# Computing one chunk's decays with one-column matmuls in place of two transfers through DRAM, in a fused recurrence and bilinear feed-forward kernel

## The chip, the cores and the metric

One core of one Trainium2 chip. The metric is the time of one launch on the device in microseconds (us). Ratios compare runs of the state "fast" alone; the medians of the table of experiments are over all timed runs, slow ones included. A "look" is one profiled execution; a look without timed rounds has the state "unknown". The profile's span is some 2 us shorter than the time of the same run.

## The reference, cut to what matters

```python
def _attn_ref(q, k, v, alpha):            # 4 x 8 heads x 768 steps x 48
    state = zeros((B, H, D, D))
    for t in range(S):
        state = alpha[:, :, t, :, None] * state + einsum('bhd,bhe->bhde', k[:, :, t], v[:, :, t])
        y[:, :, t] = einsum('bhd,bhde->bhe', q[:, :, t], state)
    return y

def _moe_ref(x, w_a, w_b, w_out):         # 3072 x 384, d_ff = 1536
    return ((x @ w_a) * (x @ w_b)) @ w_out

# the first feeds the second: x = y with heads side by side
```

The kernel cuts the 768 steps into stretches and works through six chunks (two batch rows by 256 steps each). Inside a chunk the recurrence is done by matmuls with scaled keys and queries. From one half of a chunk to the next, the state is multiplied by the half's **decay**, the product of its alphas: 48 numbers for each head. This text is about how chunk 3's decays get from where they are computed to where the state is scaled.

## The kernel before, where the change and the argument touch it

There are two routines for the same numbers. One takes them from beta (computed already) by two transfers, because they stand in two rows and are needed in columns. The other sums the logarithms again with matmuls against a column of ones, whose result already stands in columns, and takes the exponential on ScalarE:

```python
def decay(ch):                                        # "dec D"
    row = dram.tile([2, B, P2, D], F32, name="row")
    for r in range(2):
        nc.sync.dma_start(out=row[r]..., in_=ch.beta[HC - 1::HC, :, 1, ...]...)      # L213
    for r in range(2):
        nc.sync.dma_start(out=bls[ch.c % 2][r * DP:r * DP + D]..., in_=row[r]..., allow_slow_non_contiguous=True)   # L216

def decay_pe(ch):                                     # "dec P"
    s2 = bank("s2", 1, F32, [C, 2, 512])              # the one s bank
    for u in range(2):
        for hd in range(H):
            r, p = hd // P2, hd % P2
            for g in range(2):
                ...
                nc.tensor.matmul(s2[r * DP:r * DP + D, g, e:e + 1], lhsT=ch.l2[gs, u, hd, :], rhs=one[gs], start=True, stop=True)   # L228
    for r in range(2):
        nc.scalar.activation(out=bls[ch.c % 2][rs]..., in_=s2[rs, :, :2 * P2], func=AF.Exp)   # L231
```

The 32 matmuls of decay_pe are called "the burst" below. The user of the decays is the end of stK ("K"), which makes the state of the chunk's middle, Sm, and of its end, S; stS ("S") needs Sm, and stY ("Y") finishes the chunk's output, in two halves, Y0 and Y1. Y also reads m, the product with a mask that stage "D" (L273, L274) makes on VectorE:

```python
# stK: state of the chunk's middle (Sm) and of its end (S)
for g, (src, dst) in enumerate(((old, mid), (mid, new))):
    ...
    nc.vector.tensor_add(tmp[:, us], x, src)          # L341, x in PSUM (the s bank)
    eng.tensor_mul(dst, tmp[:, us], bl)               # L342, both inputs in SBUF

# stS: first half of the queries against S, second half against Sm, no wait between but for Sm
for g in range(...):
    st = Sm[...] if g else S0[...]
    ...matmul(y[...], lhsT=win(st[rs], a, t), rhs=queriesT(...))      # L291

# logs, "L": for the next chunk but one, on ScalarE and then GpSimd ("P")
nc.scalar.activation(out=x, in_=x, func=AF.Ln)        # L170
eng.tensor_add(ch.l2..., x[:, :, 0, :], x[:, :, 1, :])   # L172, reads SBUF twice
```

A plan says at which step of one chunk's feed-forward (24 half products ff_a, ff_b, then 4 outputs) a stage of another chunk is issued. The part that counts, during the feed-forward of chunk 2:

```python
2: [(1, 3, "v * S"), (3, 4, "ld a * P"), (4, 4, "ld k * P"), (5, 3, "dec D"), (6, 3, "D 0 0 y2"), (7, 3, "K * V"), (7, 4, "L * P"),
    (8, 3, "T 1 Y"), (9, 3, "S 0"), (9, 3, "D 0 1 s2"), (13, 3, "Y 0 VS"), (13, 3, "D 1 0 s2"), (14, 4, "A 0"), ...
```

Chunks 0, 1 and 2 already use "dec P", chunks 3, 4 and 5 "dec D".

## Time and profile before

| | before |
|---|---|
| time, median of the first 3 runs (range) | 219.32 us (218.82 to 219.59) |
| profiled span | 217.3 us |
| TensorE busy | 200.0 us, 92% |
| waits of TensorE after 96 us | one, 2.23 us, for Sm of chunk 3 |
| from Y1 of chunk 2 to Y0 of chunk 3 | 18.26 us |

The lines themselves are in the prediction below. The last row is the measure that I use all through: the distance between the starts of two groups of matmuls (L309 at 93.86 and at 112.12 us in the timeline of before). All that happens earlier in the run drops out of it. That matters: in the fourteen profiles of this study the first of these two groups starts anywhere from 92.73 to 95.14 us in kernels that are alike, or nearly so, up to there, so 2.4 us of the spread of these profiles comes from the first part of the run, which the change doesn't touch.

### The profile page before, as it was taken

How to read it: one execution, taken by the hardware profiler on the slowest of the kernel's cores; microseconds unless marked ns; L12 is line 12 of the kernel's file. 1: busy time of each engine (PE TensorE's matmuls, PEld its weight loads, DVE VectorE, ACT ScalarE, POOL GpSimd, SP SyncE). 2: the span in 40 equal slices, each digit the busy share in tenths (PEclk: the TensorE clock that was granted, in tenths of full speed). 3: DMA queues.
4: the chain of work that ended last, by engine and by line, in shares of the span. 5: the costliest groups of instructions: out<-in, count | busy, mean ns of one | idle time of the engine just before them, and what ended most of it. 6: DMA issues, size and time to landing. Idle time of an engine off the chain costs nothing.

```text
span 217.3 us, 6393 instructions
## 1 busy us (share of the span) xinstructions
PE 200.0 (92%) x2762; PEld 118.2 (54%) x2762; DVE 129.0 (59%) x208; ACT 119.8 (55%) x208; POOL 54.0 (25%) x66
## 2 busy tenths in 40 slices
PE   7767898999899989999599999999999999999992
PEld 7556664556565645654355555554655545544462
DVE  4668736797646879906778908559554463045500
ACT  8853276943488977248339635875433433244421
POOL 8575948029400057000620000700100000000000
PEclk9999999999999999999889999999999999999999
DMA  7999999998999355994697257595328100320023
GB/s 166 263 251 126 212 224 226 245 250 219 304 264 288 102 100 129 262 200 95 102 251 186 56 114 80 77 266 86 63 50 159 36 3 0 91 57 0 0 64 81
DMA packets 40607, 31.24 MB, mean 144 GB/s; under 512 B 29036, under 2 KB 36740, under 8 KB 40580
## 3 DMA queue, kind: packets, MB, share of 16 engines
q0 software_dynamic: 9120, 19.27, 38.8%
q1 hardware_dynamic: 31380, 11.48, 27.3%
q8 instruction: 21, 0.34, 0.7%
q10 hardware_dynamic: 80, 0.10, 0.1%
q14 instruction: 6, 0.05, 0.1%
HBM read 25.97 MB, written 4.74 MB: 141 GB/s over the span
## 4 chain that ended last, share of the span: by engine, by line
PE 69%; DMA 8%; ACT 7%; DVE 6%; SPq 3%; POOL 3%; issue 3%; DVEq 0%; ACTq 0%
PE f L382 19%; PE f L359 18%; PE f L369 17%; PE y L309 4%; PE y L291 3%; DMA k_t<-in_k_dram 3%; DVE m L274 3%; DMA wb_t<-in_moe_w_b_dram 3%; PE f L196 2%; PE s L273 2%; SPq L163 2%; ACT L170 1%; DMA bl<-row 1%; ACT a_t L170 1%; DVE QKp L207 1%
## 5 line engine op out<-in xcount | busy, mean ns | idle before, releaser
L359 PE MATMUL f<-xT,wa_t 128*128 128x512 bf16 (+1 forms) x240 | 60.2, 361 | 1.7 <-ACT as__745 L363 0.8
L369 PE MATMUL f<-xT,wb_t 128*128 128x512 bf16 (+1 forms) x240 | 60.1, 361 | 0.5 <-DMA wb_t<-in_moe_w_b_dram 0.5
L382 PE MATMUL f<-wo_t,prod 128*128 128x384 bf16 (+1 forms) x300 | 49.5, 320 | 0.0
L382 PEld LDWEIGHTS <-prod 128*128 128x128 bf16 x300 | 28.3, 98 | 18.1
L359 PEld LDWEIGHTS <-wa_t 128*128 128x128 bf16 x240 | 22.2, 98 | 24.2 <-issue 3.1
L369 PEld LDWEIGHTS <-wb_t 128*128 128x128 bf16 x240 | 22.7, 98 | 22.5 <-issue 1.7
L274 DVE TENSOR_TENSOR m<-s,mask 128x1024 bf16<-128x1024 f32 x22 | 26.9, 1222 | 6.0 <-PE s L273 5.9
L383 ACT ACTIVATE ot<-f 128x384 f32<-128x384 f32 (+1 forms) x25 | 11.9, 478 | 32.1 <-PE f L382 32.1
L172 POOL TENSOR_TENSOR l<-a_t 128x768 f32<-128x768 f32 x3 | 5.4, 1808 | 67.3 <-ACT a_t L170 67.3
L207 DVE TENSOR_TENSOR QKp<-q_t,beta 128x384 bf16<-128x384 f32 x24 | 12.9, 578 | 0.6 <-ACT beta L201 0.6
L299 ACT ACTIVATE xT<-y 128x384 bf16<-128x384 f32 (+1 forms) x12 | 7.8, 651 | 9.2 <-DVE xT L297 4.7
L207 DVE TENSOR_TENSOR QKp<-k_t,invb 128x384 bf16<-128x384 f32 x24 | 12.2, 553 | 0.2
L309 PE MATMUL y<-m,vx 64*64 64x128 bf16 x576 | 10.4, 218 | 1.7 <-DVE m L274 1.7
L309 PEld LDWEIGHTS <-vx 64*64 64x64 bf16 x576 | 8.8, 107 | 5.1 <-issue 4.9
L273 PE MATMUL s<-kqT 64*64 64x128 bf16 x352 | 10.6, 224 | 0.7 <-DVE kqT L252 0.7
L196 PE MATMUL f<-l,ut_f 128*128 128x384 f32 x24 | 9.2, 498 | 2.1 <-DVE l L172 1.1
L178 ACT ACTIVATE vx<-v_t 128x768 bf16<-128x768 f32 x10 | 8.0, 844 | 5.3 <-DMA v_t<-in_v_dram 5.3
L291 PE MATMUL y<-kqT,Sm 64*64 64x128 bf16 x144 | 6.7, 226 | 4.3 <-DVE Sm L342 2.2
L273 PEld LDWEIGHTS <-kqT 64*64 64x64 bf16 x384 | 7.6, 108 | 4.3 <-issue 2.7
L170 ACT ACTIVATE a_t<-a_t 128x1536 f32<-128x1536 f32 (+1 forms) x7 | 9.1, 1300 | 1.0 <-DMA a_t<-in_alpha_dram 0.9
L189 PE MATMUL f<-ident 128*128 128x128 bf16 x102 | 8.0, 249 | 1.4 <-POOL ident masks.py:199 1.4
L189 PEld LDWEIGHTS <-ident 128*128 128x128 bf16 x102 | 7.3, 114 | 1.5 <-POOL ident masks.py:199 1.4
(227 smaller groups left out, 267.0 us busy)
## 6 DMA issues: line engine op xcount, KB each, us to landing
out_dram<-ot SPq DMA_DIRECT2D x47, 96.0 KB, 2.2
a_t<-in_alpha_dram POOLq DMA_DIRECT2D x5, 768.0 KB, 8.5
k_t<-in_k_dram POOLq DMA_DIRECT2D x4, 768.0 KB, 12.2
q_t<-in_q_dram POOLq DMA_DIRECT2D x4, 768.0 KB, 7.5
v_t<-in_v_dram POOLq DMA_DIRECT2D x4, 768.0 KB, 10.7
wo_t<-in_moe_w_out_dram POOLq DMA_DIRECT2D x3, 384.0 KB, 10.8
a_t<-in_alpha_dram SPq DMA_DIRECT2D x2, 384.0 KB, 4.4
k_t<-in_k_dram SPq DMA_DIRECT2D x2, 384.0 KB
```

The source lines that it names most:

```text
L170: nc.scalar.activation(out=x, in_=x, func=AF.Ln)
L189: nc.tensor.matmul(w[:, :C], lhsT=ident, rhs=ident, start=True, stop=True)
L196: nc.tensor.matmul(p, lhsT=ut_f32, rhs=ch.l2[:, u].rearrange("p h d -> p (h d)"), start=True, stop=True)
L207: eng.tensor_mul(dst[ch.c % 2][:, u, :, i::2, :D], src[:, u, hs].rearrange("p a r d -> p r a d"), by[:, u, :, hs])
L273: nc.tensor.matmul(s2[g * HC:(g + 1) * HC, r, p, rk, :], lhsT=keysT(ch, u, 2 * h + p, g, r, rk), rhs=queriesT(ch, u, 2 * h + p, g, rs), st ...
L274: nc.vector.tensor_mul(m.rearrange("p r a k s -> p (r a) (k s)"), s2.rearrange("p r a k s -> p (r a) (k s)"), maskn(4))
L291: nc.tensor.matmul(y[rs, g, t * C:(t + 1) * C], lhsT=win(st[rs], a, t), rhs=queriesT(ch, u, a, g, rs), start=(n == 0), stop=False, skip_gr ...
L309: nc.tensor.matmul(ch.y[u][r * DP:(r + 1) * DP, g, t * C:(t + 1) * C], lhsT=win(vxs[ch.c % 2][gs, u, rk], a + P2 * r, t), rhs=ch.m[u, a // ...
L359: nc.tensor.matmul(ap, lhsT=wa_t[:, kk, f * 128:(f + 1) * 128], rhs=ff_x(ch, us)[:, kk], start=(kk == 0), stop=(kk == KT - 1))
L369: nc.tensor.matmul(bp, lhsT=wb_t[:, kk, f * 128:(f + 1) * 128], rhs=ff_x(ch, us)[:, kk], start=(kk == 0), stop=(kk == KT - 1))
L382: nc.tensor.matmul(op, lhsT=ch.prod[:, f, m * C:(m + 1) * C], rhs=wo_t[:, f, fs], start=(f == 0), stop=(f == NFF - 1))
L383: nc.scalar.activation(out=ot[:, fs], in_=op, func=AF.Copy)
```

## The change

Its intent: take the two transfers in series off the way to chunk 3's middle state. It is one word of the plan.

```diff
-    2: [... (4, 4, "ld k * P"), (5, 3, "dec D"), (6, 3, "D 0 0 y2"), (7, 3, "K * V"), (7, 4, "L * P"),
+    2: [... (4, 4, "ld k * P"), (5, 3, "dec P"), (6, 3, "D 0 0 y2"), (7, 3, "K * V"), (7, 4, "L * P"),
```

## The prediction

> **What bounds the kernel now.** I read the busy times and the row of slices first, then TensorE's waits from 96 us to the end, then the timeline around the one wait found there.
>
> ```profile
> PE 200.0 (92%) x2762; PEld 118.2 (54%) x2762; DVE 129.0 (59%) x208; ACT 119.8 (55%) x208; POOL 54.0 (25%) x66
> PEclk9999999999999999999889999999999999999999
> ```
>
> TensorE is busy 200.0 of 217.3 us. The clock row dips to 8 in only two slices of 5.43 us, the twentieth and the next, that is, from about 103 to 114 us. In TensorE's list of waits over the second half of the span there is one entry:
>
> ```profile
> PE y L291 <- DVE Sm L342: 2.2, 1, 2.2
> ```
>
> So TensorE sets the end, and from 96 us on it idles once, for the middle state of chunk 3 (Sm = tmp x decay). Time given back there should reach the end, as long as no new wait eats it. The timeline (start, length, engine, instruction; idle before it in brackets):
>
> ```profile
> 99.71 1.18 SPq L213 DMA_DIRECT2D row<-beta  x2
> 101.42 0.93 SPq L216 DMA_DIRECT2D bl<-row  x2
> 103.45 0.55 DVE L341 TENSOR_TENSOR tmp<-s,S 128x384 f32<-128x384 f32 x1
> 104.40 0.52 PE L291 MATMUL y<-kqT,S 64*64 64x128 bf16 x12
> 104.88 1.80 POOL L172 TENSOR_TENSOR l<-a_t 128x768 f32<-128x768 f32 x1 [19.29 <-ACT a_t L170]
> 104.97 2.12 DVE L342 TENSOR_TENSOR Sm<-tmp,bl 128x384 bf16<-128x384 f32 x1 [0.97 <-DMA bl<-row]
> 107.15 0.85 PE L291 MATMUL y<-kqT,Sm 64*64 64x128 bf16 x12 [2.23 <-DVE Sm L342]
> 107.79 0.56 DVE L342 TENSOR_TENSOR S<-tmp,bl 128x384 bf16<-128x384 f32 x1
> 108.39 1.46 PE L359 MATMUL f<-xT,wa_t 128*128 128x512 bf16 x3
> ```
>
> Three things add up. VectorE had tmp at 104.00 but waited 0.97 us for the second transfer. That delay put Sm just behind GpSimd's add (104.88 to 106.68), and Sm took 2.12 us where the next multiply of the same shape took 0.56; it ended 0.41 us after the add. And after the idle time TensorE is slow: three matmuls of L359 take 1.46 us (usually 0.81). The table by windows, whose last columns are granted clock, DMA share and GB/s, shows why:
>
> ```profile
> 106.00:107.00 1.00, 0.00 (x0) 0.00 (x0) 1.00 (x1) 0.00 (x0) 1.00 (x2) 1.00 1.16 211
> 108.00:109.00 1.00, 1.00 (x18) 0.50 (x11) 1.00 (x3) 0.00 (x0) 1.00 (x2) 0.50 0.54 63
> 110.00:111.00 1.00, 1.00 (x5) 0.42 (x4) 0.08 (x1) 0.48 (x1) 0.08 (x1) 0.73 1.05 313
> ```
>
> The clock is halved from 107.1 to about 110.5 us. So the wait costs more than its 2.23 us.
>
> **What the Trainium skill says.** "TensorE: Matmul & The Clock Gate", Part 1, says that the array's clock is halved after an idle window and comes back after about 3.4 us of work. The trace agrees on the halving and on the 3.4 us, though the idle stretch here was 2.23 us, less than a whole such window. "SBUF — State Buffer", section "SBUF: two separate sides", says that a VectorE operation with two SBUF inputs and a GpSimd operation that reads SBUF lock each other out, and whichever starts first has the port to its end. The trace agrees (2.12 against 0.56 us). [...] here issue to landing of row and bl is 3.4 us in the median, so two in series cannot be short. Removing them is right in kind.
>
> **The change part by part.** One word changes, but it moves the work: chunk 3 uses the other decay routine.
>
> *Removed:* four issues on the sync queue, the landing wait of 0.97 us and, through it, the collision.
>
> *Added on TensorE:* 32 fp32 matmuls of 64x48 by one column, which the trace splits into 64, at the place where ff_a of step 6 begins in the old program (100.50 us). The same burst for chunk 2 in the trace of before:
>
> ```profile
> 70.24 0.81 PE L359 MATMUL f<-xT,wa_t 128*128 128x512 bf16 x3
> 70.98 1.16 PE L228 MATMUL s<-one,l 64*48 64x1 f32 x64
> 72.07 0.82 PE L369 MATMUL f<-xT,wb_t 128*128 128x512 bf16 x3
> ```
>
> From its start to the next group is 1.09 us; and a group of three FF matmuls before such a burst takes 0.74 start to start, not 0.65. So it costs 1.09 + 0.09 = **1.18 us**, all on the path.
>
> *Added on ScalarE:* two exponentials, 0.178 us each by the row of L231. The order of the changed program has them after as_ of step 5 and ahead of the next as_, and no added table load. TensorE reaches the next as_ about 0.8 us after the burst, so they hide. They must also free the s bank before K (chunk 3's state products), which starts two FF groups and a D later, over 1.5 us. They hide there too.
>
> *Moved:* everything on TensorE, ScalarE and GpSimd here comes 1.18 us later. tmp then ends at 104.00 + 1.18 = 105.18, Sm follows at once and ends at about 105.72. The add starts at 104.88 + 1.18 = 106.06, so Sm misses it by 0.34 us. TensorE starts its S part at 105.58 and needs Sm 0.36 us later, at 105.94. **No wait.**
>
> *What the removed wait gave.* Before, from the S part at 104.40 to the start of Y0 (L309) at 112.12 is 7.72 us. What stands between is S and D (unstalled 1.02 us: chunk 4's, from 115.18 to the next FF group at 116.20) and four FF groups (3 x 0.65 + 0.74 = 2.69): 3.71 us. So idle and slow clock cost 7.72 - 3.71 = 4.01 us. Less 1.18, Y0 could come **2.83 us** earlier, if nothing else held it.
>
> *What is given back.* VectorE does not move with TensorE here. After Sm come the second tmp (to about 106.39) and then S = tmp x bl at 106.42, which has two SBUF inputs and now starts 0.36 us after the add. As Sm did before, it should end 0.41 us after the add: 106.68 + 1.18 + 0.41 = 108.27, beside 108.35 in the old trace. So VectorE's next operations (prod 0.68, then the mask multiply m 1.22, overlapping slightly) stand at the same absolute times as before, m ending at about 110.01. Y0 reads that m first. TensorE wanted it at 105.58 + 3.71 = 109.29; it gets it at 110.07. New waits of about 0.78 us in all appear (part of it perhaps a step earlier, at the bank that prod frees). Y0 thus comes at 110.07 instead of 112.12: **2.05 us** earlier. Later I find slack again: m of D 1 1 should end at about 115.55 and Y1 is wanted at 115.60.
>
> The sum: 4.01 - 1.18 - 0.78 = 2.05, so 219.32 - 2.05 = **217.3 us**, 0.9% faster.
>
> **The rivals.** *A: the clock drops anyway*, by its own schedule or for the thinness of the one-column bursts. Then only the 2.23 us of idle time are saved against 1.18, and with any new wait the gain is 0.3 to 1.0 us: 218.3 to 219.0. Against it: the bursts of chunks 1 and 2 ran at a clock of 1.00 before and after, and the only drop inside the run stands just behind the 2.23 us gap. A gap of 1.7 us near 56 us (L291 for tmp) left the clock at 1.00.
>
> *B: no new wait.* If S comes before the add, or VectorE's backlog is shorter than I think, the full 2.83 us stay: 216.5. For it: there are only 0.36 us between add and S in my sum, and instructions on VectorE overlap. Against it: the add hangs on a logarithm that shifts with TensorE by the same 1.18.
>
> *C: the collision only moves to Sm.* If ScalarE does its logarithm 0.4 us earlier against TensorE than I have it, the add meets Sm again; Sm would then end at about 107.9 and TensorE would idle some 2 us, perhaps with a slow clock. Then the matmuls are pure cost: up to 1.2 us slower, 220.5. Against it: ScalarE's as_ ahead of the logarithm waits for TensorE's own products.
>
> *D: a later transfer becomes the wait.* GpSimd issues the loads of chunks 4 and 5 after the add, now 1.18 us later, with users 2 us earlier. v of chunk 4 is cast at 122.98; issued at 107.79, with a landing of 10.7 us in the median, it would be there by about 119.7 after the change and wanted at about 120.9. The margin is 1.2 us; a miss on ScalarE would be a part of a microsecond, not of TensorE's time at once.
>
> **Range and chances.** B gives 216.5, my sum 217.3, A 218.3 to 219.0, C 220.5 with a small chance. The three timed runs span 0.8 us. A range of 216.2 to 218.5 should hold it 8 times in 10. A gain above 2% needs 214.9, more than all of idle time and slow clock less the matmuls: 2 in 100. A loss above 2% needs 223.7: 1 in 100.
>
> **What would show it right or wrong.** In the changed profile: L228 has 64 more matmuls on TensorE and L213 and L216 have eight issues, not twelve; the wait of L291 for Sm is gone; Sm takes 0.56 us and S of chunk 3 about 1.9; the clock row stays at 9; and L309 of chunk 3 shows a new wait of 0.4 to 0.8 us for m. A clock that still dips makes A right; S at 0.56 us and no wait of L309 makes B right; Sm again at 2 us makes C right. A TensorE wait traced to a load after 115 us would mean D, and none of my sums.

## The result, and the profile after

| | before | after |
|---|---|---|
| time, median | 219.07 us (4 runs, 217.99 to 219.59) | 216.58 us (4 runs, 216.55 to 217.09) |
| ratio, 95% interval | | 0.990 (0.986 to 0.994) |
| profiled span | 217.3 us | 214.7 us |
| from Y1 of chunk 2 to Y0 of chunk 3 | 18.26 us | 16.23 us |
| from Y0 of chunk 3 to the end | 105.2 us | 104.9 us |

A ratio here is the mean time of one kernel's fast runs over that of the other's in the same rounds, so it isn't quite the ratio of the medians. By the 2% rule this is "the same": the change gains 1.0%.

TensorE's granted clock in slices, and its list of waits from 96 us to the end, after:

```profile
PEclk9999999999999999999999999999999999999999
```
```profile
PE y L309 <- DVE m L274: 0.3, 1, 0.3
```

The dip in the clock row is gone, the wait for Sm is gone, and a small wait that was not there before has come: Y0 (L309) for the mask multiply m. The timeline of the changed kernel at the same place:

```profile
100.33 1.16 PE L228 MATMUL s<-one,l 64*48 64x1 f32 x64
101.54 0.37 ACT L231 ACTIVATE bl<-s 48x16 f32<-48x16 f32 x2 [1.15 <-PE s L228]
104.97 0.56 DVE L342 TENSOR_TENSOR Sm<-tmp,bl 128x384 bf16<-128x384 f32 x1
105.69 0.50 PE L291 MATMUL y<-kqT,Sm 64*64 64x128 bf16 x12
105.81 1.81 POOL L172 TENSOR_TENSOR l<-a_t 128x768 f32<-128x768 f32 x1 [20.48 <-ACT a_t L170]
106.22 1.82 DVE L342 TENSOR_TENSOR S<-tmp,bl 128x384 bf16<-128x384 f32 x1
108.56 1.21 DVE L274 TENSOR_TENSOR m<-s,mask 128x1024 bf16<-128x1024 f32 x1
109.82 0.86 PE L309 MATMUL y<-m,vx 64*64 64x128 bf16 x48 [0.33 <-DVE m L274]
```

Sm now takes 0.56 us and is over at 105.53, before GpSimd's add begins at 105.81. The S half of the same pair of products runs into the add instead and takes 1.82 us; the mask multiply stands behind it, and Y0 behind that.

So of 2.6 us between the two profiles, 2.03 us lie in the stage of the change. The rest is not the change's: 0.27 us were there before it (the first group starts at 93.59 against 93.86 us), and 0.2 to 0.3 us lie after it, where the list of waits of neither kernel's TensorE has an entry.

### The profile page after: what moved, and what is told of

Read it like the earlier page. It is cut to its first block, busy times and chain, and to the rows that moved or that the text cites. A ratio compares the mean times of both kernels' runs of the same rounds, so it can differ in the third digit from the quotient of the medians.

```text
span 214.7 us, 6515 instructions
## 1 busy us (share of the span) xinstructions
PE 199.4 (93%) x2826; PEld 118.5 (55%) x2826; DVE 128.4 (60%) x208; ACT 120.2 (56%) x210; POOL 54.0 (25%) x66
## 4 chain that ended last, share of the span: by engine, by line
PE 67%; DMA 11%; DVE 6%; ACT 6%; issue 3%; SPq 2%; POOL 2%; ACTq 0%; DVEq 0%
PE f L382 19%; PE f L359 17%; PE f L369 17%; DMA a_t<-in_alpha_dram 5%; PE y L309 4%; DVE m L274 3%; DMA wa_t<-in_moe_w_a_dram 3%; DMA k_t<-in_k_dram 3%; PE y L291 3%; PE f L196 3%; SPq L163 2%; PE s L273 2%; ACT L170 1%; DVE QKp L207 1%; PE s L228 1%
## 5 line engine op out<-in xcount | busy, mean ns | idle before, releaser
L359 PE MATMUL f<-xT,wa_t 128*128 128x512 bf16 (+1 forms) x240 | 59.6, 358 | 2.0 <-ACT as__745 L363 1.2
L309 PE MATMUL y<-m,vx 64*64 64x128 bf16 x576 | 10.3, 218 | 2.0 <-DVE m L274 2.0
L309 PEld LDWEIGHTS <-vx 64*64 64x64 bf16 x576 | 8.9, 107 | 5.4 <-issue 5.2
L291 PE MATMUL y<-kqT,Sm 64*64 64x128 bf16 x144 | 6.1, 217 | 2.0 <-DVE tmp L341 2.0
```

Of the source, the lines that this page charges most:

```text
L291: nc.tensor.matmul(y[rs, g, t * C:(t + 1) * C], lhsT=win(st[rs], a, t), rhs=queriesT(ch, u, a, g, rs), start=(n == 0), stop=False, skip_gr ...
L309: nc.tensor.matmul(ch.y[u][r * DP:(r + 1) * DP, g, t * C:(t + 1) * C], lhsT=win(vxs[ch.c % 2][gs, u, rk], a + P2 * r, t), rhs=ch.m[u, a // ...
L359: nc.tensor.matmul(ap, lhsT=wa_t[:, kk, f * 128:(f + 1) * 128], rhs=ff_x(ch, us)[:, kk], start=(kk == 0), stop=(kk == KT - 1))
```

## The experiments

All runs were correct. The first column of times is the stage measure from the profile of that run, the second is from the same start to the end of the span; ratios are to the kernel before in the same rounds. The end is taken from a span printed to 0.1 us, so the distances to the end hold to 0.05 us. The rule for slow runs (over 1.5% above the fastest) leaves out 4 of 35 and 10 of 43 timed runs of before in the two large calls; the third look at before, 221.03 us, lies where those do. Part of before's slow course is thus left out of the ratios, which may understate a gain.

| run | Y1 chunk 2 to Y0 chunk 3 | to the end | median us | ratio (95%) |
|---|---|---|---|---|
| before (three looks) | 18.26 / 15.32 / 18.69 | 123.44 / 122.48 / 123.86 | 218.85 and 219.05 | |
| the change (two looks) | 16.23 / 16.23 | 121.11 / 121.12 | 216.58 and 216.99 | 0.990, 0.989 |
| e1: before, add later | 15.94 | 121.14 | 216.66 | 0.990 (0.984 to 0.995) |
| e2: before, transfers early (two looks) | 15.03 / 15.03 | 121.23 / 121.87 | 217.48 | 0.995 (0.993 to 0.998) |
| e3: e1 and e2 together | 14.49 | 119.65 | 215.38 | 0.985 (0.981 to 0.989) |
| e4: the change, add later | 15.69 | 120.56 | 217.50 | 0.990 (0.985 to 0.995) |
| e5: before, wait filled | 17.01 | 122.23 | 218.18 | 0.999 (0.996 to 1.002) |
| e6: the change, burst twice | 17.83 | 123.33 | 218.94 | 1.000 (0.998 to 1.003) |
| e7: the change, chunks 4 and 5 too | 16.23 | 124.13 | 219.91 | 1.007 (1.004 to 1.009) |
| e12: e3, chunk 2 by transfers | 14.49 | 119.58 | 214.51 | 0.980 (0.976 to 0.983) |

My theory: the change wins the wait for Sm, which was made of a late transfer, a locked port and a slow clock, and pays 1.18 us for the burst and something for S. Rivals: only the transfer counts; the clock drops anyway; the matmuls are cheaper than transfers as such.

### e1: the transfers stay, GpSimd's add moves away

```diff
-(7, 3, "K * V"), (7, 4, "L * P"), (8, 3, "T 1 Y"), (9, 3, "S 0"),
+(7, 3, "K * V"), (8, 3, "T 1 Y"), (9, 3, "S 0"), (9, 4, "L * P"),
```

> The kernel before, with the logarithm and the add of chunk 4 (L, add on GpSimd) moved from step 7 to step 9, behind S 0 of chunk 3. The transfers of chunk 3's decays stay as they are, no matmuls are added. My theory: the wait of TensorE for Sm was 0.97 us of transfer and 1.56 us of the port held by the add (2.12 against 0.56 us), and only their sum brought the half clock. So Sm should take 0.56 us, TensorE's wait shrink from 2.23 to about 0.7 us, the clock stay at 1.00, and Y0 of chunk 3 come 2.8 us earlier: about 216.3 us, ratio 0.987. Rival (the transfers alone are the loss, the add does no harm): the wait stays near 2.2 us and the time at 219.1 us, ratio 1.00.

Timeline of this run:

```profile
105.39 0.56 DVE L342 TENSOR_TENSOR Sm<-tmp,bl 128x384 bf16<-128x384 f32 x1 [1.49 <-DMA bl<-row]
106.00 0.52 PE L291 MATMUL y<-kqT,Sm 64*64 64x128 bf16 x12 [1.17 <-DVE Sm L342]
107.29 1.80 POOL L172 TENSOR_TENSOR l<-a_t 128x768 f32<-128x768 f32 x1 [21.80 <-ACT a_t L170]
```

The edit moves the whole stage L, the logarithm on ScalarE as well as the add. The transfer landed even later than in the first look at before (VectorE waited 1.49 us, not 0.97), yet Sm took 0.56 us and TensorE waited 1.17 us in place of 2.23, and there was no half clock behind it. The stage is 2.32 us shorter, which is more than the change itself won there, without touching the decays. I had expected 2.8; the later landing is most of the difference (a wait of 1.17 in place of 0.7). **The rival that only the transfer counts is out**: the add on GpSimd was the larger half of the wait.

### e2: the transfers stay, but earlier

```diff
-(22, 2, "T 1 Y"), (23, 4, "new")   ...   (5, 3, "dec D"),
+(22, 2, "T 1 Y"), (22, 3, "dec D"), (23, 4, "new")
```

> The kernel before, with the two transfers of chunk 3's decays issued some 17 us earlier on the sync queue (when chunk 3's decays have long been computed), no matmuls. My theory: the transfers were late only because of where they stood in the queue; early, they cost nothing, and TensorE saves the 1.18 us of the burst as well. Sm starts right after tmp and ends before the add starts; S is still blocked by the add, so about 0.6 to 0.8 us is given back: Y0 3.2 us earlier than before, about 215.9 us, ratio 0.985, and 0.6 to 1.2 us faster than the changed kernel. Rival (the matmuls are needed, since transfers land late or delay the sync queue's transposes): no better than 216.6 us, and a new wait for a transpose or still for bl.

In both looks the stage took 15.03 us, 3.23 less than the slow course of before, where I had expected 3.2, and no wait for bl is left. Sm starts right after tmp, and S meets the add (1.82 us), as in the changed kernel. So the transfers cost nothing once they are issued in time: what made them late was their place in the sync queue, where before issues them at 99.71 us, right behind six output transfers (95.91 to 99.65 us). But the times are only 0.5% better than before, not 1.5%. The timeline shows where the rest went:

```profile
115.48 0.58 PE L309 MATMUL y<-m,vx 64*64 64x128 bf16 x27
116.88 0.52 PE L309 MATMUL y<-m,vx 64*64 64x128 bf16 x21 [0.81 <-issue]
```

TensorE stood still in the middle of Y1 of chunk 3, after 27 of its 48 matmuls, and "issue" means that the profile knows of nothing it waited for. More on that below.

### e3: both

The edits of e1 and e2 together.

> Transfers early and the add of chunk 4 two steps later, in one kernel, no matmuls. My theory: neither Sm nor S of chunk 3 meets the add, so all of idle time and slow clock, 4.01 us, is saved but for some 0.2 us of latency at the s bank: about 215.3 us, ratio 0.983. No wait of TensorE over 0.3 us between 96 us and the end. Rival (VectorE's backlog holds Y0 whatever the add does): same as with the transfers early alone, about 215.9 us.

```profile
103.82 0.56 DVE L342 TENSOR_TENSOR Sm<-tmp,bl 128x384 bf16<-128x384 f32 x1
105.07 0.56 DVE L342 TENSOR_TENSOR S<-tmp,bl 128x384 bf16<-128x384 f32 x1
107.18 1.81 POOL L172 TENSOR_TENSOR l<-a_t 128x768 f32<-128x768 f32 x1 [21.80 <-ACT a_t L170]
108.14 0.86 PE L309 MATMUL y<-m,vx 64*64 64x128 bf16 x48
```

Neither product meets the add, TensorE's list of waits from 90 us to the end is empty, and the stage is 3.77 us shorter than the slow course of before. The time is 215.38 us against 215.3 expected. That is below the changed kernel's 216.58 and 216.99 us, though in other rounds and with intervals that overlap; in the stage it is 1.74 us ahead. This is the size of what idle time and slow clock had cost in that course: 3.77 us, where the prediction had 4.01.

### e5: the wait filled with useless work

```diff
+            if (ch.c, u, g) == (3, 0, 0):             # in stS, between the S half and the Sm half
+                for _ in range(36):
+                    nc.tensor.matmul(y[:, 0, KT * C:], lhsT=ident, rhs=ident, start=False, stop=False, ...)
```

> The kernel before, with 36 dummy matmuls (128x128 by 128, 0.056 us each, about 2.0 us) in an unused quarter of the y bank between the S half and the Sm half of S 0 in chunk 3. They do no useful work and fill the wait; Sm comes no sooner. My theory: the half clock comes from the idle time, so TensorE's granted clock stays at 1.00 through 110 us and the 1.7 us that the slow clock cost are saved: about 217.4 us, ratio 0.992, Sm still taking 2.1 us. Rival A (the clock drops by its own schedule): still half clock from 107 to 110.5 us, and the time stays at 219.1 us or above.

Its timeline, and two windows behind the filled gap (after the window, its length and the busy times of the five engines, TensorE first and its weight loads second, comes the granted clock):

```profile
104.86 2.18 PE L296 MATMUL y<-ident 128*128 128x128 bf16 x36
105.30 1.82 DVE L347 TENSOR_TENSOR Sm<-tmp,bl 128x384 bf16<-128x384 f32 x1 [1.29 <-DMA bl<-row]
110.88 0.86 PE L314 MATMUL y<-m,vx 64*64 64x128 bf16 x48
```
```profile
107.00:108.00 1.00, 0.74 (x25) 0.53 (x28) 0.86 (x3) 0.00 (x0) 1.00 (x2) 1.00 0.00 0
109.00:110.00 1.00, 1.00 (x7) 0.47 (x5) 1.00 (x1) 0.60 (x1) 1.00 (x1) 1.00 0.72 199
```

The Sm half starts at 107.17 us, as in before (107.15), but the clock stays at 1.00 and Y0 comes at 110.88 and not 112.12. From the Sm half to Y0 are 3.71 us against 4.97: **the slow clock alone cost 1.26 us**, and here it did not come once the idle time was filled. The timed runs agree: none of the 14 has a mean granted clock below 0.989, while 8 of the 35 of before in the same rounds lie at 0.984 or below. The 1.26 us are less than the 1.7 us that half a clock for 3.4 us would make, because a part of that stretch is a wait for the s bank, which the clock doesn't lengthen. The times don't resolve it: 0.67 us better in the median, a ratio of 0.999, where 0.992 was expected. A likely reason came out in the next pair.

### e9 and e10: the kernel before, looked at again

> The kernel before, unchanged, for a second look. The mean granted clocks of its timed runs lie in three heaps, about 1.00, 0.99 and 0.98, as if each execution had none, one or two half-clock stretches of 3.4 us. Theory: the gap of 2.23 us at chunk 3 is there in every execution, but the half clock follows it in some two of three only. In this look either the clock drops behind the gap (then from the Sm half to Y0 takes 4.97 us as in the first) or it does not (then about 3.7 us, as with the dummy matmuls). Rival: it always drops there, and the heaps come from elsewhere.

> The kernel before, unchanged, a third look, for the same question: the wait of 2.2 us for Sm again in any case; behind it either a half clock and 4.97 us from the Sm half to Y0, or clock 1.00 and 3.7 us.

The second look has another course than the first. Its timeline:

```profile
104.71 0.56 DVE L342 TENSOR_TENSOR Sm<-tmp,bl 128x384 bf16<-128x384 f32 x1 [0.75 <-DMA bl<-row]
104.84 2.10 POOL L172 TENSOR_TENSOR l<-a_t 128x768 f32<-128x768 f32 x1 [19.29 <-ACT a_t L170]
105.32 0.52 PE L291 MATMUL y<-kqT,Sm 64*64 64x128 bf16 x12 [0.44 <-DVE Sm L342]
116.93 0.52 PE L309 MATMUL y<-m,vx 64*64 64x128 bf16 x21 [1.73 <-issue]
```

The transfer landed 0.2 us sooner, Sm got the port 0.13 us ahead of the add, and this time it was the add that was held (2.10 in place of 1.80 us). TensorE waited 0.44 us, the clock stayed, and the stage took 15.32 us, less than with the change. Then 1.73 of it were lost again to the same kind of standstill in Y1 as in e2. My expectation, a gap of 2.2 us in every execution, was **wrong**: whether it comes is decided by a fraction of a microsecond between a landing transfer and an add.

The third look has the slow course again: Sm waited 1.78 us for its transfer, then met the end of the add and took 1.32 us in place of 0.56:

```profile
107.06 1.32 DVE L342 TENSOR_TENSOR Sm<-tmp,bl 128x384 bf16<-128x384 f32 x1 [1.78 <-DMA bl<-row]
108.43 0.52 PE L291 MATMUL y<-kqT,Sm 64*64 64x128 bf16 x12 [2.23 <-DVE Sm L342]
```

The half clock came here too, from 109.90 us on. The trace's records of the clock show a part of its rule: in all fourteen profiles every stretch of full clock lasts a whole multiple of 3.413 us, and every half clock inside a run lasts one such window. In both slow looks, the window just ahead of the drop holds most of the 2.2 us of idle time (the window from 103.7 to 107.1 us holds 2.2 us of it in the first look, that from 106.5 to 109.9 us holds 1.9 in the third). A longer gap, 2.69 us in e2 (32.58 to 35.28 us, for ScalarE), is cut by a window's edge into 0.8 and 1.9 us and left the clock at 1.00. So it seems to matter how a gap lies to the windows. But that is not the whole rule. All fourteen profiles have a gap of 1.60 to 1.88 us near 14 to 16 us (L291 waiting for tmp). In six of them (e1, e3, e4, e5, e9, e10) the clock is halved in the next window, in eight it is not, and where the gap lies to the windows doesn't sort them: it lies wholly inside a window in e5, with a drop, and in e11 and e12, without one. What decides there stays open.

The mean granted clocks of the 78 timed runs of before in the two large calls fit that: 10 lie at 0.996 or above, 44 between 0.988 and 0.992, 24 at 0.984 or below. One half window in 217 us is worth 0.008, so I read these as none, one and two drops; the early one near 16 to 18 us, in the part before the change, accounts for the clock of 0.99 in kernels without a gap at chunk 3. None of the ten timed runs of the changed kernel lies below 0.992; e1 and e4, which have no long gap at chunk 3 in their profiles, have one run each at 0.983 and 0.982, both slow, which I can't explain. That reading is inferred; only the profiles show where a drop lay.

### e0, e4, e6, e7: what the change pays

The changed kernel again, as a mark:

> The changed kernel itself again, as a mark for the other three of this call: 216.6 us, ratio to before 0.989.

It took 216.99 us (ratio 0.989), and 16.23 us in the stage, to the hundredth the same as in its first look, and e7 has the same. So in three looks the changed kernel's stage does not vary as before's does.

e4 moves the add in the changed kernel, with the edit of e1:

> The changed kernel, with the logarithm and the add of chunk 4 at step 9 in place of 7. My theory: what the changed kernel gives back comes from S of chunk 3 being held by the add (1.82 us) and the mask multiply behind it. So S takes 0.56 us, the waits of Y0 (0.33 us) and of the FF group ahead of it go, and Y0 comes about 0.5 us earlier: about 216.1 us, ratio to before 0.987. Rival (the waits come from VectorE's load anyhow): no change, 216.6 us, Y0 still waits for m.

The stage is 0.54 us shorter (15.69) and the end comes 0.55 us sooner, as expected; VectorE holds Y0 no more:

```profile
105.97 0.56 DVE L342 TENSOR_TENSOR S<-tmp,bl 128x384 bf16<-128x384 f32 x1
109.03 0.86 PE L309 MATMUL y<-m,vx 64*64 64x128 bf16 x48
```

So **0.54 us is what the change gave back through S**, where the prediction had 0.78. The expected time, 216.1 us, was not met (217.50): the timed runs of this kernel spread from 215.75 to 220.0 us (the last a slow run) and cannot tell it from the mark.

e6 issues the burst twice:

```diff
-        for u in range(2):
+        for u in (0, 1, 0, 1) if ch.c == 3 else (0, 1):
```

> The changed kernel, with chunk 3's 32 decay matmuls issued twice over (same values). My theory: the burst lies wholly on the path, so a second one costs 1.09 us more (64 records more): about 217.7 us, ratio to before 0.994. Rival (it is hidden in waits that follow, such as Y0's): the second costs under 0.5 us.

The stage is 1.60 us longer, not 1.09, and the median 1.95 us above the mark (1.83 by the fast runs alone). The second burst itself added 0.86 us to the next group (1.95 from 100.40 to 102.35 in place of 1.09). The burst does lie on the path, so the rival is out; but my number missed a second effect. Timeline and windows of this run:

```profile
100.40 2.02 PE L228 MATMUL s<-one,l 64*48 64x1 f32 x128
```
```profile
101.00:102.00 1.00, 1.00 (x89) 1.00 (x86) 0.27 (x1) 0.00 (x0) 0.00 (x0) 1.00 1.12 209
104.00:105.00 1.00, 1.00 (x36) 0.51 (x38) 1.00 (x2) 1.00 (x1) 0.00 (x0) 0.50 0.57 123
```

TensorE was busy throughout, and still the clock fell to 0.50 from 103.9 us for one window of 3.4 us. The window ahead of the drop (100.45 to 103.86, TensorE busy for 3.36 of its 3.41 us) is the one with the 128 one-column matmuls. So **two microseconds of one-column matmuls looked to the clock like idle time** in this look, whereas the single burst of 1.1 us did no such thing in two looks at the changed kernel, one at e4 and one at e7. It doesn't happen each time: 6 of this kernel's 22 timed runs have a mean clock of 0.996 or above, hence no drop.

e7 goes the other way and uses matmuls for chunks 4 and 5 too:

```diff
-(27, 4, "dec D")            -(13, 5, "dec D")
+(27, 4, "dec P")            +(13, 5, "dec P")
```

> The changed kernel, with the decays of chunks 4 and 5 by matmuls too. Their transfers show no wait in the trace, so my theory is that each burst is pure cost, 1.18 us: about 2.3 us slower, 218.9 us, ratio to before 0.999. Rival (matmuls are better than transfers as such, or the queue's relief helps): at or below 216.6 us.

```profile
145.52 1.16 PE L228 MATMUL s<-one,l 64*48 64x1 f32 x64 [0.58 <-DVE m L274]
```

The end comes 3.02 us later, the median 2.9 us, and the kernel is slower than before (1.007). Chunk 4's burst cost 1.19 us, as expected. Chunk 5's cost 1.86: the s bank it writes was still held by a mask multiply, and TensorE waited 0.58 us for it. So the matmuls are not better as such; they are worse wherever a transfer is in time.

### e11: the standstill again

> The kernel with the transfers issued early, unchanged, for a second look. In its first look TensorE stood still for 0.81 us in the middle of Y1 of chunk 3, with no wait named. If that belongs to this kernel (where its instructions stand, or the loads at that time), it is there again and from Y1 of chunk 2 to the end takes 121.2 us; if it was chance, it is gone and takes 120.4 us.

It came again, at the same place (after 27 matmuls of Y1), 1.48 us long, and the end came after 121.9 us. So it belongs to this kernel. It was seen in four looks: e2, e11, the second at before, and e6, where it took 0.39 us:

```profile
116.98 0.58 PE L309 MATMUL y<-m,vx 64*64 64x128 bf16 x27
117.95 0.52 PE L309 MATMUL y<-m,vx 64*64 64x128 bf16 x21 [0.39 <-issue]
```

All four reach Y1 of chunk 3 (at 113.2 to 117.0 us) with the loads of chunks 4 and 5 filling the DMA engines. In each, a packet of 16 KB on the queue of kind "instruction" had started shortly before, in the midst of those loads, and the matmuls went on 2.5 to 2.8 us after that packet's start (e11 2.54, e6 2.71, e2 2.75, e9 2.77). The two slow looks at before come to the same matmul 3.6 and 4.0 us after such a packet's start, and don't stand still. The place fits too: the queue moves 21 packets for 5524 records of TensorE in before, some 263 to a packet if it serves TensorE (an estimate), and e6's two bursts are 256 records, about one packet. So e6 meets the same matmul at the same place in a packet as before does, and the changed kernel, with one burst, does not; it has no standstill. That speaks for late instructions, but **no experiment settles it**: the profile names no releaser, and I moved neither the loads nor the instructions by themselves. (In e1 and e3 the loads are later, and the standstill is gone, which fits too.)

### e12: the best kernel, and chunk 2's burst taken away

```diff
-(12, 2, "dec P")        # on top of e3
+(12, 2, "dec D")
```

> The kernel with transfers early and the add later, and chunk 2's decays by transfers too, in the place in the queue where the burst stood. Theory (a burst costs its 1.18 us only where no later wait takes it up): after chunk 2's burst TensorE waits 1.03 us for GpSimd's add of chunk 3, which hangs on ScalarE, not on the burst; so the gain is 0.4 us at most, about 215.1 us, and less if the transfers land after tmp of chunk 2. Rival (each burst removed gives 1.18 us): 214.2 us.

From Y1 of chunk 1 to Y1 of chunk 2 it took 35.29 us, against 36.02 in e3: 0.73 us won, between the two expectations (0.4 at most, 1.18). The wait that I said would take up the burst is there but shorter:

```profile
PE f L196 <- POOL l L172: 0.7, 1, 0.7
```

In e3 the same line says 1.0: ScalarE and GpSimd came somewhat sooner too, which I had not allowed for. With 214.51 us, ratio 0.980 (0.976 to 0.983), this kernel is 2.0% faster than before (by the 2% rule "unclear", since the interval spans 2%). It was timed neither against the changed kernel nor against e3 in the same rounds.

## Why the prediction was right, point by point

- **What bounds the kernel.** Right. What was won in the stage stayed won to the end: 2.03 us at Y0 and 2.3 us at the end in the profiles.
- **The cost of the burst, 1.18 us.** Right. In the changed kernel it takes 1.09 us to the next group (100.33 to 101.42) and the group ahead of it 0.74 us; chunk 4's in e7 cost 1.19. What the sum did not have is that such a burst also seems to count little towards the clock: once it was harmless, twice it was not (one look, e6).
- **The exponentials hidden.** Right: they end at 101.91, and K starts at 103.28 without a wait.
- **Sm misses the add.** Right, by 0.28 us where I had 0.34.
- **Idle time and slow clock, 4.01 us.** The mechanism was right, the term a little large: 3.77 us by e3. What was mis-sized is S and D without a stall, 1.02 us as read off chunk 4; in e3 they take 1.25 us (104.19 to 105.44).
- **S runs into the add, and Y0 waits.** Right, with 1.82 us for S where I had about 1.9, and 0.54 us given back where I had 0.78 (e4). The two errors are 0.24 us each and cancel, but not by luck: the prediction had Y0 wait for VectorE's m at 110.07 us, so the time at which TensorE itself would be ready drops out of the sum. What the 2.05 rests on is VectorE's chain, and that came within 0.04 us: counted from the same Y1, S ended at 108.31 (predicted 108.27) and m at 110.04 (predicted 110.01).
- **The transfers.** Two readings were off. The 3.4 us "of row and bl" is the landing of one bl transfer, that of chunk 5; the trace has none for row. The argument needs only that two in series are long, and there row was issued at 99.71 us and Sm had bl at 104.97. Early issue (e2) made that length harmless.
- **Rivals.** A (the clock drops anyway) is out by e3 and e5 for the single burst; its second form, the thin bursts, came true once the burst was doubled (e6). The gap of 1.7 us that the prediction put near 56 us stands at 14.25 to 15.97 us, and as evidence it is weak: behind the same gap the clock did drop in six of the fourteen profiles. B (no new wait) is out by the wait of Y0 and by e4, though it was near: half a microsecond. C (Sm meets the add again) did not come. D (a later load becomes the wait) did not come in the changed kernel, but a standstill beside those loads did in others.
- **What it did not see.** It took one trace of before for the kernel. Before has two courses, 18.3 to 18.7 us and 15.3 us in the stage, by whether Sm or the add gets the port first. The 2.03 us hold against the slow course; against the fast one the changed kernel is 0.91 us behind at Y0, and ahead at the end only because that look lost 1.73 us to the standstill. The measured 1.0% is a mean over both, so that it agrees with a 0.9% read from one slow look is in part luck. The time came out 0.7 us below my 217.3 (216.58), within the range; most of this is the start and the end of the run, outside the stage.
- **The larger point.** The prediction asked what the matmuls cost against the transfers, and not whether the transfers had to be late. The better answer to the same wait was to issue them some 15 us earlier and to move the add (e3): the burst's 1.18 us and the 0.54 us given back are saved as well.

## What to carry to other kernels

When a wait ends in a transfer, look first at where the transfer stands in its queue and when its data was ready; if it could have gone long before, moving the issue is cheaper than replacing it with work on the engine that sets the end. Look then at what the delayed operation ran into: here a late landing of 1 us became a wait of 2.2 us and a loss of 3.8 us, through a port shared with GpSimd and a halved clock. And take a second profile before you trust a gap in the first, for an order that a tenth of a microsecond decides is not a property of the kernel.

## What the Trainium skill lacked or had wrong

- "TensorE: Matmul & The Clock Gate", "Why this matters for your kernels", advises against idle gaps of over about 3 us. Here shorter ones went before a halved clock: 1.9 and 2.2 us of idle time within one window of 3.413 us at chunk 3, and a gap of 1.71 to 1.88 us near 16 us in six of fourteen profiles. A gap of 1.17 us (e1) and one of 2.69 us cut by a window's edge (e2) did not. The window of 3413 ns that its Part 1 gives is what the clock records show.
- The same page does not say what one-column matmuls count for. In e6 some 2 us of them (128 records of fp32, 64x1), with 0.05 us of idle time in the window, were followed by a clock of 0.50 for 3.4 us; 1.1 us of them were not.
- "SBUF — State Buffer", "SBUF: two separate sides", says that the second comer is blocked for the whole instruction. The runs agree, and in both orders: the VectorE product took 1.32 to 2.12 us in place of 0.56 behind the add, the add 2.10 in place of 1.80 behind the product. The page lacks a size for this pair: the product ended 0.41 to 0.42 us after the add.
- "DMA: Bandwidth & Descriptors", "Anatomy of one DMA", gives a fixed cost of about 2 us, nearly constant, for the path through GpSimd; it lacks one for transfers from the sync queue. For those of 3 KB here, where the trace has the landing, issue to landing was 2.0 us at the least (e3) and 5.9 us at the most (e2).
- "Runtime: NRT & Kernel Launch", "Instruction fetch mechanics", has no standstill of TensorE in mid-group, without a branch and without any wait named: 0.39, 0.81, 1.48 and 1.73 us in four looks, beside loads that filled the DMA engines, each over 2.5 to 2.8 us after a packet of kind "instruction" started. Its cause stays open.
